# Byte offsets of TensorE's operands: activations, gate halves and split keys placed at a different offset modulo 256 in each chunk, step or pair of heads

## The chip, the cores and the metric

The kernel runs on one core of one Trainium2 chip. The metric is the device time of one execution in microseconds; the time before is the median of three runs, 678.17 us (676.92 to 685.84). The profile is one execution taken by the hardware profiler, and its span, 676.2 us, runs from the first to the last instruction.

## What is computed

Sliding-window attention with four sink keys, and behind it a two-matrix feed-forward with the gate h - tanh(h). Everything is float32.

```python
batch, n_heads, seq, head_dim = (4, 8, 768, 64)      # n_sink 4, window 128
scores = matmul(q, k.transpose(0, 1, 3, 2)) / sqrt(64)
keep = is_sink | ((rel >= 0) & (rel < window))       # rel = query position - key position
a = softmax(where(keep, scores, -1e9))
x = matmul(a, v).transpose(0, 2, 1, 3).reshape(3072, 512)
h = x @ w_in                                          # 512 x 2048
out = (h - tanh(h)) @ w_out                           # 2048 x 512
```

## The kernel before

**Tiles and stages.** The 3072 rows are cut into 12 chunks of 256 rows, and the feed-forward's 2048 columns into 8 groups of 256. A step is one chunk and one group; there are 96 steps, in an order of which chunks 0 to 2 share the first 24 (n = 0 to 23) and chunks 3 to 11 follow with eight steps each (n = 24 to 95). Attention for a chunk is done in four units, one for each pair of heads, some steps ahead of the chunk's first step.

**Split operands.** Products that have to be exact to float32 are made of single-pass products: a value is written as a high half, rounded to float32r, and a low half, the rest. A float32r product is one matmul instruction where a plain float32 product of the scores or values is two.

**The matmuls of a step.** `first_half` (mm1, L807) makes h: 24 matmuls of 128x128 stationary by 256 moving columns. Stationary is a block of w_in, from the resident tiles `w` for chunks 0 to 2, and from a ring of streamed blocks (`ring` and `spare`) for chunks 3 to 11. Moving is the chunk's activations, high half xh or low half xl, which lie in one tile `xall` (two places, by `home(cc)`) except for chunk 2, which has two tiles xh and xl of its own. `gate` (L826 to L848) takes h through tanh on ScalarE, the difference on VectorE, and writes the gate's two halves into `ghbuf` (ScalarE, L832 or L845) and `glbuf` (VectorE, L835 or L848). `second_half` multiplies them by w_out, and TensorE has the gate's halves as stationary and w_out as moving. For chunks 0 to 4 and for the last step these are 12 matmuls of 512 columns (mm2, L877). For chunks 5 to 11 they are 21 matmuls of 256 columns (mm7, L911), the seven products of a Strassen scheme on sums of the gate's and the weights' quarters.

**The attention's matmuls.** From unit 12 on, scores are two float32r passes over 260 columns (L524): moving is `ks`, the split keys of the pair, stationary is `q`. The other attention matmuls are plain float32: transposes of 128 columns (L609), and the values (L672).

**Order.** A planner (`Work`) fixes the order of all instructions of all engines from durations, due times and the resources that each piece of work names; ("gl", n % 2) is the name of a step's low half in `glbuf`. On TensorE the order is step n's L807, then step n - 1's L877 or L911, with pieces of attention between them.

**Where the operands lie.** A tile's place in SBUF, counted in bytes from its partition's start, follows from the pools. In the built program before, modulo 256: all of `w`, the Strassen weights `edge` and `w_out` blocks lie at 0, except the tile that holds w_in group 1 and later the ring, at 64 (`FAR`). `spare`, `ghbuf`, `glbuf` and `q` lie at 64. `xall` is read at 0 for chunks 3 to 11, and at 64 for chunks 0 and 1 (the `16 * (cc < 3)` in `x_high`). Chunk 2's xh is at 64 and its xl at 0. `ks` is read at 0 and 128 for the first half of a unit's queries and at 16 and 144 for the second.

```python
at = 2 * NPAIR * CH * (1 - home(cc)) + 16 * (cc < 3)
both = xall[:, at : at + 2 * NPAIR * CH].rearrange("p (k n c) -> p k n c", k=2, n=NPAIR)
```

Of the kernel before, what the change touches and what calls it, by code (L numbers as in the profile page):

```python
# [39 lines left out]
@with_exitstack  # L40
def kernel(
    ctx: ExitStack,
    tc: tile.TileContext,
    qd: bass.AP,
    kp: bass.AP,
    vp: bass.AP,
    vs: bass.AP,
    nsw: bass.AP,
    w_in: bass.AP,
    w_out: bass.AP,  # L50
    xd: bass.AP,
    out: bass.AP,
):
    nc = tc.nc

    cpool = ctx.enter_context(tc.tile_pool(name="cpool", bufs=1))
    ident = cpool.tile([P, P], F32, tag="ident", name="ident")
    nswi = cpool.tile([P, 32], I32, tag="nswi", name="nswi")[:, :4]

    pts = cpool.tile([P, NPAIR, 2, 4, P], F32, tag="pt", name="pt")  # L60
    early = []
    for m in range(2):
        first = pts[:, m].rearrange("p h a b -> p (h a b)")
        early.append((first[:, :KW], first[:, KW : KW + 2 * CH].rearrange("p (h s) -> p h s", h=2)))
    et = mybir.EngineType
    with tc.manual_schedule(engines={et.PE, et.SP, et.DVE, et.Activation, et.Pool}):

        scr = pts[:, 2, 0]
        nc.sync.dma_start(nswi, nsw.partition_broadcast(P))
        for m in range(2):  # L70
            k, q = early[m]
            nc.sync.dma_start(k, kp[0, m, :, :KW])
            _load_pair(nc, q, qd[0, 2 * m : 2 * m + 2, :, :CH], True)
            if m == 0:
                make_identity(nc, ident)
                nc.gpsimd.iota(scr[:, 0, :].bitcast(I32), pattern=[[-1, P]], base=0, channel_multiplier=1)
                nc.gpsimd.iota(scr[:, 1, :].bitcast(I32), pattern=[[1, P]], base=0, channel_multiplier=0)
        masks = _masks(nc, cpool, nswi, scr)
        _, (nlo, nhi, wlo, whi) = nc.values_load_multi_w_load_instructions(
            nsw[0:1, 0:4], skip_runtime_bounds_check_because="every value takes one of the two branches"  # L80
        )
        bad = nhi | whi | ((nlo + 3) >> 3) | ((wlo - 1) >> 7)


        WARM = 3
        with tc.tile_pool(name="warm", bufs=1, space=PSUM) as wp:
            warm = wp.tile([P, P], F32, tag="warm", name="warm")
            for _ in range(WARM):
                nc.tensor.matmul(warm, lhsT=ident, rhs=ident, start=True, stop=True)

    with tc.If(bad == 0) as cmp:
        _banded(tc, qd, kp, vp, vs, masks, w_in, w_out, ident, pts, early, out)
    with cmp.Else():
        _general(tc, qd, kp, vp, nswi, w_in, w_out, ident, xd, out)

# [8 lines left out]
        nc.sync.dma_start(q[r, h, :], src[h, r])  # L104


def _masks(nc, pool, nswi, scr):

    mask = pool.tile([P, 3, TS], F32, tag="mask", name="mask")
    above = pool.tile([P, P], F32, tag="above", name="above")
    below = pool.tile([P, P], F32, tag="below", name="below")
    after = pool.tile([P, P], F32, tag="after", name="after")
    lim = pool.tile([P, 2], F32, tag="lim", name="lim")
    diff, col, tmp = (scr[:, i, :] for i in range(3))
    nc.gpsimd.memset(mask[:, 0, :NSK], NEG)
    nc.vector.tensor_copy(diff, diff.bitcast(I32))
    nc.vector.tensor_copy(col, col.bitcast(I32))  # L120
    nc.vector.tensor_scalar(above, diff, 0.0, None, op0=ALU.is_lt)
    nc.vector.tensor_scalar(below, diff, 0.0, None, op0=ALU.is_le)
    nc.vector.tensor_scalar(after, diff, 0.0, None, op0=ALU.is_gt)
    nc.vector.scalar_tensor_tensor(diff, above, float(P), diff, op0=ALU.mult, op1=ALU.add)
    nc.vector.tensor_scalar(tmp, above, NEG, None, op0=ALU.mult)
    nc.vector.tensor_copy(lim[:, 0:1], nswi[:, 0:1])
    nc.vector.tensor_copy(lim[:, 1:2], nswi[:, 2:3])
    n_sink, window = lim[:, 0:1], lim[:, 1:2]
    nc.vector.tensor_scalar(mask[:, 2, NSK:], diff, window, NEG, op0=ALU.is_ge, op1=ALU.mult)
    nc.vector.tensor_scalar(col, col, n_sink, NEG, op0=ALU.is_ge, op1=ALU.mult)  # L130
    nc.vector.tensor_tensor(mask[:, 0, NSK:], mask[:, 2, NSK:], tmp, op=ALU.min)
    nc.vector.tensor_tensor(mask[:, 0, NSK:], mask[:, 0, NSK:], col, op=ALU.max)

    near, edge, sink = diff[:, :NSK], tmp[:, :NSK], col[:, :NSK]
    nc.vector.tensor_scalar(near, near, window, None, op0=ALU.is_lt)
    nc.vector.tensor_tensor(edge, edge, near, op=ALU.mult)
    nc.vector.tensor_tensor(mask[:, 1, :NSK], edge, sink, op=ALU.min)

    def rest():
        nc.scalar.copy(mask[:, 1, NSK:], mask[:, 2, NSK:])  # L140
        nc.scalar.copy(mask[:, 2, :NSK], sink)

    return mask, above, below, after, rest
# [86 lines left out]
        return sorted(start, key=lambda n: (start[n], n)), start  # L230


def _banded(tc, qd, kp, vp, vs, masks, w_in, w_out, ident, pts, early, out):
    nc = tc.nc
    et = mybir.EngineType
    with ExitStack() as ctx:
# [6 lines left out]
        bpool, wmpool, qpool, kpool, hpool, xpool = (  # L243
            pool(n, 1) for n in ("bpool", "wmpool", "qpool", "kpool", "hpool", "xpool")
        )
        pp, sm = pool("pp", 2), pool("sm", 4)
        xall = xpool.tile([P, 4 * NPAIR * CH + 16], F32R, tag="xall", name="xall")
        ps, ps_h = pool("ps", 1, space=PSUM), pool("ps_h", 2, space=PSUM)
        dpool = pool("dpool", 1, space=bass.MemoryType.DRAM)

        banks = {n: ps.tile([P, 512], F32, tag=n, name=n) for n in ("s0", "s1", "o0", "o1", "t", "x")}
# [4 lines left out]
        flat = wide.rearrange("p a b c -> p (a b c)")  # L256
        gbuf = gpool.tile([P, 8, P], F32, tag="gbuf", name="gbuf")
        ghbuf = gpool.tile([P, 2, 7, P], F32R, tag="ghbuf", name="ghbuf")
        glbuf = gpool.tile([P, 8, P], F32R, tag="glbuf", name="glbuf")
        wscr = dpool.tile([NG, P, 2 * WG], F32, tag="wscr", name="wscr")  # L260
        bscr = dpool.tile([NG, P, 5, DM // 2], F32, tag="bscr", name="bscr")
        kscr = dpool.tile([2, P, 2, DM // 2], F32, tag="kscr", name="kscr")
# [33 lines left out]
        def home(cc):  # L296

            return cc if cc < 3 else cc % 2

        def raw(u):  # L300
            return u < RAW
# [111 lines left out]

        sides = cpool.tile([P, 4], F32, tag="sides", name="sides")
        sidei = cpool.tile([P, 16], I32, tag="sidei", name="sidei")[:, :4]
        half, odd = sides[:, 0:2], sides[:, 2:4]
        vsink = cpool.tile([P, 2, P], F32R, tag="vsink", name="vsink")
        vraw = cpool.tile([P, P], F32, tag="vraw", name="vraw")  # L420
# [53 lines left out]
        def split(u):  # L474

            def k_high(h):
                if h == 0:
                    t = hpool.tile([P, NPAIR * CH], F32R, tag="ha", name=f"ks{u}")  # L480
                    ks[u] = t[:, : 2 * (KW + 24)].rearrange("p (h k) -> p h k", h=2)[:, :, :KW]
                r = slice(64 * h, 64 * h + 64)
                nc.scalar.copy(ks[u][r, h, :], kt[u][r, :])  # L483

            def k_low(h):
                k, t = ks[u], kt[u]
                r, o = slice(64 * h, 64 * h + 64), slice(64 * (1 - h), 64 * (1 - h) + 64)
                (nc.gpsimd if KP else nc.vector).tensor_tensor(k[o, h, :], t[r, :], k[r, h, :].bitcast(F32), op=ALU.subtract)  # L488

            def q_high():  # L490
                t = bpool.tile([P, 2, 2, CH], F32R, tag="hb", name=f"q{u}")
                qh[u], ql[u] = t[:, 0], t[:, 1]
                nc.scalar.copy(qh[u], qt[u])

            def q_low():
                (nc.gpsimd if QP else nc.vector).tensor_tensor(ql[u], qt[u], qh[u].bitcast(F32), op=ALU.subtract)  # L496

            t = due_unit(u) - 5000
            k, q = ([s] for s in slots(u))
            old = [("x", 2)] + [("xu", 2, i) for i in range(NPAIR)] if u == 3 * NPAIR else []  # L500
            work.add("ACT", 525, t, q_high, q, ["qh"] + old)
            work.add("POOL" if QP else "DVE", 1360 if QP else 705, t, q_low, q + ["qh"], ["ql"], port=True)
            for h in range(2):
                work.add("ACT", 425, t, lambda h=h: k_high(h), k, [("ks", h)] + old)
                work.add("POOL" if KP else "DVE", 1050 if KP else 590, t, lambda h=h: k_low(h), k, [("ks", h)], port=True)

        def scores(u, t):
# [21 lines left out]
            def merge():  # L529
                ps = sps[u, t]  # L530
                if t == 0:
                    if slot(u) > 1:
                        pr[u] = wide[:, slot(u) - 2]
                    else:
                        pr[u] = pp.tile([P, 4, TS], F32, tag="p", name=f"p{u}")
                    st[u] = sm.tile([P, 12], F32, tag="st", name=f"st{u}")
                for h in range(2):
                    if kind > 0:
                        nc.vector.copy_predicated(ps[h][:, TS:WIN], above.bitcast(U32), ps[h][:, :P])
# [102 lines left out]
        def attend(cc, p0, pairs):  # L642
# [35 lines left out]
            def x_high(i):  # L678
                if p0 == 0 and i == 0:
# [1 line left out]
                        xh[cc] = bpool.tile([P, NPAIR, CH], F32R, tag="hb", name=f"xh{cc}")  # L681
                        xl[cc] = hpool.tile([P, NPAIR, CH], F32R, tag="ha", name=f"xl{cc}")
                    else:
                        at = 2 * NPAIR * CH * (1 - home(cc)) + 16 * (cc < 3)
                        both = xall[:, at : at + 2 * NPAIR * CH].rearrange("p (k n c) -> p k n c", k=2, n=NPAIR)
                        xh[cc], xl[cc] = both[:, 0], both[:, 1]
                r = slice(p0 + 2 * i, p0 + 2 * i + 2)
# [126 lines left out]

        def halves(n):
            r = n % 2
            return ghbuf[:, r].rearrange("p b t -> p (b t)")[:, : 2 * CH], glbuf.rearrange("p b t -> p (b t)")[:, r * 2 * CH : (r + 1) * 2 * CH]

        def gate(n):
            g0 = gbuf.rearrange("p b t -> p (b t)")[:, : 2 * CH]  # L820
# [542 lines left out]
```

## Time and profile before

| | |
|---|---|
| time, median of 3 runs | 678.17 us (676.92 to 685.84) |
| the profiled execution: its span | 676.2 us |
[...]
| matmul records | 5099 |
| HBM traffic over the span | 225 GB/s |

The profile gives no time of its own for the profiled execution beside its span; the median of the runs is 1.97 us above it. A matmul's recorded duration is the time from its start until its last result; matmuls overlap in the pipeline, so the rate at which TensorE works is not read from the duration but from the distance between starts, and where a row merges several matmuls, from the start of the next row less the start of this one, divided by the count.

### The profile page before, as it was taken

Reading aid. Unit: us, or ns where it says so; the run is one execution under the profiler, and the core shown is the slowest. Engines: PE = TensorE matmul, PEld = TensorE weight load, DVE = VectorE, ACT = ScalarE, POOL = GpSimd, SP = SyncE. Lnnn points to the kernel's source line nnn. Section 1 sums busy time; section 2 is a strip of 40 time slices with the busy share of each in tenths; the row PEclk is TensorE's granted clock in tenths of the full one; section 3 lists DMA queues with packets and bytes.
Section 4 is the critical chain, followed back from the end, with each engine's and each line's share of the span. In section 5 each row is a group of like instructions: output and inputs, shape, how many; then the busy total and the mean of one; then the engine's idle time right before and its main releaser. Section 6 shows DMA issues by size and latency. Waiting matters only on the chain.

```text
span 676.2 us, 14570 instructions
## 1 busy us (share of the span) xinstructions
PE 655.5 (97%) x5099; PEld 603.3 (89%) x5099; DVE 531.8 (79%) x1365; ACT 412.6 (61%) x1056; POOL 204.0 (30%) x363
## 2 busy tenths in 40 slices
PE   6899999999999999999999999999999999999995
PEld 4677899998988899889999999999999999999995
DVE  6889998964898975567798898888988878855654
ACT  4986443435998876556776667567667567632331
POOL 5454000001995443344523323332223322300100
PEclk9999999999999999999999999999999999999998
DMA  5878797786998677799977767867777766657861
GB/s 177 266 262 269 266 295 263 270 287 175 191 203 274 203 217 223 227 280 266 300 217 240 224 199 207 260 196 203 227 231 216 242 199 199 198 165 207 270 198 37
DMA packets 79341, 152.96 MB, mean 226 GB/s; under 512 B 9564, under 2 KB 25564, under 8 KB 79260
## 3 DMA queue, kind: packets, MB, share of 16 engines
q1 hardware_dynamic: 65884, 121.65, 57.4%
q0 software_dynamic: 13376, 30.30, 16.4%
q8 instruction: 42, 0.69, 0.4%
q14 instruction: 39, 0.32, 0.1%
HBM read 131.47 MB, written 20.45 MB: 225 GB/s over the span
## 4 chain that ended last, share of the span: by engine, by line
PE 73%; ACT 7%; DVE 5%; DMA 5%; POOL 4%; issue 4%; POOLq 0%; SPq 0%; DVEq 0%; ACTq 0%
PE h L807 30%; PE s L911 10%; PE o L911 7%; PE o L877 6%; PE x L672 3%; PE s L877 3%; DMA w<-bscr 2%; PE t L609 2%; PE t L672 2%; PE t L877 2%; PE t L524 2%; PE x L877 2%; ACT p L575 2%; PE x L524 1%; ACT p L549 1%
## 5 line engine op out<-in xcount | busy, mean ns | idle before, releaser
L807 PE MATMUL h<-xall,ring 128*128 128x256 f32 x990 | 130.9, 279 | 0.0
L807 PEld LDWEIGHTS h<-xall,ring 128*128 128x128 f32 x990 | 121.2, 188 | 0.9 <-PE t L672 0.2
L826 ACT ACTIVATE gbuf<-h 128x512 f32<-128x512 f32 x96 | 57.1, 595 | 84.6 <-PE h L807 55.2
L356 POOL DMA_DIRECT2D qraw<-qd x36 | 29.3, 813 | 222.4 <-DVE q L496 198.0
L807 PE MATMUL h<-xall,spare 128*128 128x256 f32 x738 | 96.2, 277 | 0.0
L807 PEld LDWEIGHTS h<-xall,spare 128*128 128x128 f32 x738 | 90.0, 188 | 0.5
L549 ACT ACTIVATE p<-p,st 128x132 f32<-128x132 f32 x168 | 66.9, 400 | 26.8 <-DVE st L541 25.5
L845 ACT CAST ghbuf<-gbuf 128x896 fp32r<-128x896 f32 x55 | 51.9, 943 | 49.3 <-DVE gbuf L842 48.8
L848 DVE TENSOR_TENSOR glbuf<-gbuf,ghbuf 128x896 fp32r<-128x896 f32 x55 | 60.3, 1096 | 19.7 <-ACT ghbuf L845 16.0
L575 ACT ACTIVATE p<-p,st 128x132 f32<-128x132 f32 x168 | 54.2, 394 | 3.9 <-DVE st L570 3.5
L829 DVE TENSOR_TENSOR gbuf<-h,gbuf 128x512 f32<-128x512 f32 x55 | 37.8, 687 | 19.1 <-ACT gbuf L826 18.7
L877 PE MATMUL o<-w,ghbuf 128*128 128x512 f32 x192 | 50.8, 399 | 0.3
L629 POOL TENSOR_TENSOR pt<-pt,after 128x512 f32<-128x512 f32 x32 | 44.4, 1386 | 22.0 <-ACT pt L626 21.3
L807 PE MATMUL h<-xall,w 128*128 128x256 f32 x384 | 50.5, 282 | 0.0
L807 PEld LDWEIGHTS h<-xall,w 128*128 128x128 f32 x384 | 48.5, 188 | 1.6
L829 DVE TENSOR_TENSOR h<-h,gbuf 128x512 f32<-128x512 f32 x41 | 28.5, 694 | 19.1 <-ACT gbuf L826 19.0
L488 DVE TENSOR_TENSOR ks<-kraw,ks 64x392 fp32r<-64x392 f32 x72 | 40.4, 562 | 3.4 <-ACT ks L483 1.1
L877 PEld LDWEIGHTS o<-w,ghbuf 128*128 128x128 f32 x192 | 33.8, 188 | 6.8 <-ACT ghbuf L832 0.9
L623 DVE TENSOR_TENSOR pt<-t,below 128x512 f32<-128x512 f32 (+1 forms) x48 | 28.8, 600 | 12.6 <-PE t L609 7.4
L483 ACT CAST ks<-kraw 64x392 fp32r<-64x392 f32 x72 | 37.1, 515 | 2.2 <-DMA kraw<-kp 1.4
L911 PE MATMUL s<-edge,ghbuf 128*128 128x256 f32 x220 | 35.5, 280 | 0.1
L835 DVE TENSOR_TENSOR glbuf<-h,ghbuf 128x512 fp32r<-128x512 f32 x41 | 28.1, 685 | 9.1 <-ACT ghbuf L832 9.1
(174 smaller groups left out, 1560.8 us busy)
## 6 DMA issues: line engine op xcount, KB each, us to landing
ring<-wscr SPq DMA_DIRECT2D x165, 256.0 KB, 4.3
spare<-wscr SPq DMA_DIRECT2D x123, 256.0 KB, 4.6
qraw<-qd POOLq DMA_DIRECT2D x36, 256.0 KB, 5.0
wraw<-w_in SPq DMA_DIRECT2D x16, 512.0 KB, 6.0
wraw<-w_out SPq DMA_DIRECT2D x16, 512.0 KB, 5.7
wscr<-w SPq DMA_DIRECT2D x16, 512.0 KB, 6.0
kraw<-kp POOLq DMA_DIRECT2D x36, 196.0 KB, 4.6
v<-vp POOLq DMA_DIRECT2D x18, 256.0 KB, 3.4
```

The source lines that it names most:

```text
L483: nc.scalar.copy(ks[u][r, h, :], kt[u][r, :])
L488: (nc.gpsimd if KP else nc.vector).tensor_tensor(k[o, h, :], t[r, :], k[r, h, :].bitcast(F32), op=ALU.subtract)
L549: nc.scalar.activation(e, e, AF.Exp, bias=st[u][:, j : j + 1], scale=-1.0, accum_out=st[u][:, 4 + j : 5 + j],)
L575: nc.scalar.activation(pr[u][:, j, :], pr[u][:, j, :], AF.Copy, scale=s[:, 8 + j : 9 + j])
L629: nc.gpsimd.tensor_tensor(w[:, :, 0, :], w[:, :, 0, :], after.unsqueeze(1).to_broadcast([P, 4, P]), op=ALU.mult)
L807: nc.tensor.matmul(hps[n][:, f, :], lhsT=w, rhs=x, start=r == 0, stop=r == 11)
L826: nc.scalar.activation(g0, h(), AF.Tanh)
L829: nc.vector.tensor_tensor(g0 if strassen(n) else h(), h(), g0, op=ALU.subtract)
L845: nc.scalar.copy(ghbuf[:, n % 2], gbuf[:, 1:, :])
L848: nc.vector.tensor_tensor(glbuf[:, :7, :], gbuf[:, 1:, :], ghbuf[:, n % 2].bitcast(F32), op=ALU.subtract)
L877: nc.tensor.matmul(sums_of(n, cc, t), lhsT=a[:, f, t * P : (t + 1) * P], rhs=wt[1, g][:, (0, 1, 0)[i], f, :], start=first and not low and ...
L911: nc.tensor.matmul(acc, lhsT=a[:, b, :], rhs=factor(g, m, part % 2), start=g == 0 and part == 0 and m in (4, 1, 2, 7), stop=closes(n) and ...
```

## The change

No instruction is added, removed or moved: on every engine the same operations stand in the same order. What changes is where operands lie.

- **Activations**, `xoff(cc)`: `xall` is read, in bytes modulo 256, at 192 for chunk 0, 160 for 1, 0 for 3 (as before), 192 for 4, 16 for 5, 176 for 6, 32 for 7, 160 for 8, 48 for 9, 112 for 10 and 0 for 11 (as before). Chunk 2 is not in `xall`. The stationary blocks that go with them stay at 64, or 0 and 64 for chunks 0 and 1.
- **The gate's halves** of the 512-column steps, `shift(n)`: `ghbuf` and `glbuf` are used 0, 32, 64, 96 or 128 bytes further on, by n modulo 5. The moving weights stay at 0. The Strassen steps keep 64 and 0.
- **Split keys**: `ks` of unit u begins 32 * (u % 8) bytes further on, and the second head of the pair lies a multiple of 256 bytes behind the first, so that TensorE reads them at 32 * (u % 8) and 16 more.
- To make room, `lim`, `sides`, `sidei` and one of the four `st` buffers move into the unused columns of the tile of `nswi`, the other `st` share one tile, and `glbuf` moves to another pool and grows by 128 bytes.

```diff
-        xall = xpool.tile([P, 4 * NPAIR * CH + 16], F32R, tag="xall", name="xall")
+        SHIFT, XOFF = 32, 48
+        xall = xpool.tile([P, 4 * NPAIR * CH + XOFF], F32R, tag="xall", name="xall")
...
+        stats = sm.tile([P, 3, 12], F32, tag="st", name="st")
+        glflat = cpool.tile([P, SHIFT + 8 * P], F32R, tag="glbuf", name="glbuf")
+        glbuf = glflat[:, : 8 * P].rearrange("p (b t) -> p b t", b=8)
...
+        def xoff(cc):
+            return (48, 40, 0, 0, 48, 4, 44, 8, 40, 12, 28, 0)[cc]
+
+        def shift(n):
+            return (0, 8, 16, 24, 32)[n % 5]
...
-                    ks[u] = t[:, : 2 * (KW + 24)].rearrange("p (h k) -> p h k", h=2)[:, :, :KW]
+                    o = 8 * (u % 8)
+                    ks[u] = t[:, o : o + 896].rearrange("p (h k) -> p h k", h=2)[:, :, :KW]
...
-                    st[u] = sm.tile([P, 12], F32, tag="st", name=f"st{u}")
+                    st[u] = stats[:, u % 4] if u % 4 < 3 else small[:, 20:32].bitcast(F32)
...
-                        at = 2 * NPAIR * CH * (1 - home(cc)) + 16 * (cc < 3)
+                        at = 2 * NPAIR * CH * (1 - home(cc)) + xoff(cc)
...
             r = n % 2
-            return ghbuf[:, r].rearrange("p b t -> p (b t)")[:, : 2 * CH], glbuf.rearrange("p b t -> p (b t)")[:, r * 2 * CH : (r + 1) * 2 * CH]
+            a, b = shift(n), shift(n) + r * 2 * CH
+            return ghbuf[:, r].rearrange("p b t -> p (b t)")[:, a : a + 2 * CH], glflat[:, b : b + 2 * CH]
```

One thing follows from the last hunk. The low halves of two steps in a row lay side by side in `glbuf`; with shifts that differ they overlap by up to 32 columns, so the write of one can have to wait until TensorE has read the other. The order of VectorE's low halves (L835 before, L847 now) from step 4 on, first in the kernel before:

```order
244 L835 TENSOR_TENSOR glbuf<-h_1050,ghbuf 128x512 [waits Activation_49]
...
247 L835 TENSOR_TENSOR glbuf<-h_1101,ghbuf 128x512 [waits Activation_49]
...
253 L835 TENSOR_TENSOR glbuf<-h_1157,ghbuf 128x512 [waits Activation_49]
```

and in the changed one, at the same places:

```order
244 L847 TENSOR_TENSOR glbuf<-h_1036,ghbuf 128x512 [waits Activation_49]
...
247 L847 TENSOR_TENSOR glbuf<-h_1087,ghbuf 128x512 [waits PE_49,Activation_49]
...
253 L847 TENSOR_TENSOR glbuf<-h_1143,ghbuf 128x512 [waits PE_49,Activation_49]
```

Nothing moved; 15 of the 41 low halves of this form have a wait for TensorE (PE) more.

## Rows read from the trace of the kernel before

**Rows 1.** The page: span, and busy time of TensorE and VectorE
```profile
span 676.2 us, 14570 instructions
...
PE 655.5 (97%) x5099; PEld 603.3 (89%) x5099; DVE 531.8 (79%) x1365; ACT 412.6 (61%) x1056; POOL 204.0 (30%) x363
```

**Rows 2.** The page: the chain that ended last, by engine and by line
```profile
PE 73%; ACT 7%; DVE 5%; DMA 5%; POOL 4%; issue 4%; POOLq 0%; SPq 0%; DVEq 0%; ACTq 0%
PE h L807 30%; PE s L911 10%; PE o L911 7%; PE o L877 6%; PE x L672 3%; PE s L877 3%; DMA w<-bscr 2%; PE t L609 2%; PE t L672 2%; PE t L877 2%; PE t L524 2%; PE x L877 2%; ACT p L575 2%; PE x L524 1%; ACT p L549 1%
```

**Rows 3.** Waits of TensorE, longest first: total us, times, longest
```profile
PE s L517 <- DMA qk<-qd: 3.3, 2, 1.7
PE warm L89 <- POOL pt L103: 3.2, 1, 3.2
```

**Rows 4.** Line 807: duration ns min/median/max, first and last start us
```profile
L807 PE MATMUL h<-xall,ring x990: 276/276/388, 205.0 to 663.5; 128*128 128x256 f32 x198
...
L807 PE MATMUL h<-xall,spare x738: 276/276/374, 209.1 to 662.8; 128*128 128x256 f32 x185
...
L807 PE MATMUL h<-xall,w x384: 276/279/472, 42.6 to 192.7; 128*128 128x256 f32 x192
```

**Rows 5.** The chain in order of time: start us, us, what
```profile
98.88 2.86 PE h L807 x24
...
104.53 2.83 PE h L807 x24
...
159.06 2.80 PE s L877 x12
...
364.32 3.40 PE h L807 x30
```

**Rows 6.** Timeline of TensorE, 595 to 600 us: start us, us, instructions
```profile
594.98 1.52 PE L807 MATMUL h<-xall,ring 128*128 128x256 f32 x12
596.34 0.84 PE L807 MATMUL h<-xall,spare 128*128 128x256 f32 x6
597.02 0.62 PE L911 MATMUL s<-edge,ghbuf 128*128 128x256 f32 x4
...
599.40 0.84 PE L807 MATMUL h<-xall,spare 128*128 128x256 f32 x6
```

**Rows 7.** Timeline of TensorE, 489 to 496 us
```profile
489.71 3.09 PE L807 MATMUL h<-xall,ring 128*128 128x256 f32 x24
492.64 0.40 PE L524 MATMUL t<-ks,q 128*128 128x260 f32 x2
...
493.12 0.63 PE L911 MATMUL s<-edge,ghbuf 128*128 128x256 f32 x4
493.59 0.39 PE L911 MATMUL o<-edge,ghbuf 128*128 128x256 f32 x2
493.81 0.62 PE L911 MATMUL s<-w,ghbuf 128*128 128x256 f32 x4
...
494.72 0.40 PE L524 MATMUL t<-ks,q 128*128 128x260 f32 x2
...
495.21 0.41 PE L911 MATMUL s<-edge,glbuf 128*128 128x256 f32 x2
```

**Rows 8.** Timeline of TensorE, 143 to 147 us, steps of 512 columns
```profile
143.37 0.63 PE L877 MATMUL x<-w,glbuf 128*128 128x512 f32 x2
143.84 2.03 PE L877 MATMUL s<-w,ghbuf 128*128 128x512 f32 x8
145.70 0.63 PE L877 MATMUL s<-w,glbuf 128*128 128x512 f32 x2
```

**Rows 9.** Timeline of VectorE, the same stretch
```profile
143.66 0.68 DVE L835 TENSOR_TENSOR glbuf<-h,ghbuf 128x512 fp32r<-128x512 f32 x1
144.27 1.21 DVE L735 TENSOR_TENSOR w<-pt,w 128x1024 fp32r<-128x1024 f32 x1
```

More of the change, by code (lines that the diff above doesn't have):

```diff
@@ L57 @@
     ident = cpool.tile([P, P], F32, tag="ident", name="ident")
-    nswi = cpool.tile([P, 32], I32, tag="nswi", name="nswi")[:, :4]
+    small = cpool.tile([P, 32], I32, tag="nswi", name="nswi")
+    nswi = small[:, :4]
     pts = cpool.tile([P, NPAIR, 2, 4, P], F32, tag="pt", name="pt")
@@ L77 @@
                 nc.gpsimd.iota(scr[:, 1, :].bitcast(I32), pattern=[[1, P]], base=0, channel_multiplier=0)
-        masks = _masks(nc, cpool, nswi, scr)
+        masks = _masks(nc, cpool, small, scr)
         _, (nlo, nhi, wlo, whi) = nc.values_load_multi_w_load_instructions(
@@ L91 @@
     with tc.If(bad == 0) as cmp:
-        _banded(tc, qd, kp, vp, vs, masks, w_in, w_out, ident, pts, early, out)
+        _banded(tc, qd, kp, vp, vs, small, masks, w_in, w_out, ident, pts, early, out)
     with cmp.Else():
@@ L104, in _load_pair, with _masks @@
         nc.sync.dma_start(q[r, h, :], src[h, r])
-def _masks(nc, pool, nswi, scr):
+def _masks(nc, pool, small, scr):
     mask = pool.tile([P, 3, TS], F32, tag="mask", name="mask")
@@ L115, in _masks @@
     after = pool.tile([P, P], F32, tag="after", name="after")
-    lim = pool.tile([P, 2], F32, tag="lim", name="lim")
+    nswi, lim = small[:, :4], small[:, 4:6].bitcast(F32)
     diff, col, tmp = (scr[:, i, :] for i in range(3))
@@ L230, in order, with _banded @@
         return sorted(start, key=lambda n: (start[n], n)), start
-def _banded(tc, qd, kp, vp, vs, masks, w_in, w_out, ident, pts, early, out):
+def _banded(tc, qd, kp, vp, vs, small, masks, w_in, w_out, ident, pts, early, out):
     nc = tc.nc
@@ L245, in _banded @@
         )
-        pp, sm = pool("pp", 2), pool("sm", 4)
-        xall = xpool.tile([P, 4 * NPAIR * CH + 16], F32R, tag="xall", name="xall")
+        pp, sm = pool("pp", 2), pool("sm", 1)
+        SHIFT, XOFF = 32, 48
+        xall = xpool.tile([P, 4 * NPAIR * CH + XOFF], F32R, tag="xall", name="xall")
         ps, ps_h = pool("ps", 1, space=PSUM), pool("ps_h", 2, space=PSUM)
+        stats = sm.tile([P, 3, 12], F32, tag="st", name="st")
+        glflat = cpool.tile([P, SHIFT + 8 * P], F32R, tag="glbuf", name="glbuf")
+        glbuf = glflat[:, : 8 * P].rearrange("p (b t) -> p b t", b=8)
         dpool = pool("dpool", 1, space=bass.MemoryType.DRAM)
@@ L258, in _banded @@
         ghbuf = gpool.tile([P, 2, 7, P], F32R, tag="ghbuf", name="ghbuf")
-        glbuf = gpool.tile([P, 8, P], F32R, tag="glbuf", name="glbuf")
         wscr = dpool.tile([NG, P, 2 * WG], F32, tag="wscr", name="wscr")
@@ L412, in _banded @@
             qt[u], kt[u] = q, k
-        sides = cpool.tile([P, 4], F32, tag="sides", name="sides")
-        sidei = cpool.tile([P, 16], I32, tag="sidei", name="sidei")[:, :4]
+        sides = small[:, 8:12].bitcast(F32)
+        sidei = small[:, 16:20]
         half, odd = sides[:, 0:2], sides[:, 2:4]
```

## The prediction, made before the changed kernel ran

> **What bounds the kernel now.** I read the page's busy times first: TensorE is busy 655.5 of 676.2 us [rows 1], so little of its time is idle. Then the chain that ended last: 73% of it is TensorE, and 30% of the span is line 807 alone [rows 2]. Then TensorE's waits: the two longest totals are 3.3 and 3.2 us [rows 3]. So for most of the span the kernel lasts as long as TensorE takes to work off its queue, and a change of the time per matmul passes into the end nearly one to one. VectorE, busy 531.8 us [rows 1], is next.
>
> Since no instruction moves, the question is whether the time per matmul depends on where its operands lie. Durations give the first sign: line 807 shows 276 ns at least everywhere, and 276 is also the median on `ring` and `spare`, but on `w` the median is 279 [rows 4]. The distances between starts say more. With moving data at 0 and stationary at 64 (modulo 256), 30 matmuls in a row take 3.40 us, 113.3 ns each [rows 5]; so do the 18 from 594.98 to 597.02 (2.04 us) and the 21 of line 911 behind them, up to 599.40 (2.38 us) [rows 6]. With moving at 64 and stationary at 0, the 24 at 104.53 take 2.83 us, 117.9 ns; with both halves at different places (chunk 2: 64 and 0, against 0), the 24 at 98.88 take 2.86 us, 119.2 ns [rows 5]. [...]
>
> The good level isn't held by the placing alone. At 489.71, behind the attention's value products, 24 matmuls at the good offsets take 2.93 us, 122.1 ns; behind four of line 524, the next four of line 911 take 0.47 us, 117.5 ns, and the two after them 0.22 us, 110 ns by the row's two decimals [rows 7]. So TensorE has to fall into the good level after a disturbance, mostly within a handful of matmuls, sometimes only after a whole step. I read this as a lock between the two operands' reads that exists at 0 against 64, and that no row here shows at another placing.
>
> **The change, part by part.**
>
> *Activations, chunks 4 to 10*: 7 chunks x 8 steps x 24 = 1344 matmuls of line 807 leave the good placing. Upper bound from rows of matmuls with the operands elsewhere: 122.5 ns, the four of line 524 from 494.72 to 495.21 with moving at 16 and 144 [rows 7] (their 260 columns make them 1.6% longer by themselves, 120.6 ns for 256). Nearer is the range 117.9 to 119.2 ns of line 807 itself [rows 5]. Lower bound: the best that any row shows, 113.3. I take 118, near the row of the same form: 118 - 113.3 = 4.7 ns more for those that are at the good level now. That is not all of them; the median of 276 ns in rows 4 says over half, rows 6 and 7 show steps of either kind, and I estimate 0.8. So 1344 x 0.8 x 4.7 ns = 5.1 us. Bounds: from 1344 x 0.2 x -4.7 = -1.3 us (every one comes to the good level) to 1344 x (120.6 - 113.3) x 0.9 = +8.8 us, and with a price that no row shows, more (a rival below).
>
> *Line 911* keeps its own offsets, but now each of its groups follows matmuls that are out of step. Rows 7 show the price of falling in again, 4 x (117.5 - 113.3) = 17 ns; over the 48 steps of chunks 5 to 10 that is 0.8 us. Bounds 0 and, if the lock is not found in 21 matmuls, 48 x 21 x 4.5 ns = 4.5 us.
>
> *Chunks 0 and 1*: 384 matmuls go from 64 to 192 and 160. Chunk 0 then has the same distance between its operands as the good placing (192 - 0, as 0 - 64), so it could gain 192 x 4.6 ns = 0.9 us; chunk 1 I leave as it is. Since each step there is broken by matmuls of 512 columns, I take -0.2, with bounds of -1.8 (both chunks gain) and +0.9 us.
>
> *Gate halves, 480 matmuls of 512 columns less those at shift 0*: now 232.5 ns (eight in 1.86 us) [rows 8] to 233.3 ns (twelve in 2.80) [rows 5]. Twice the two levels of 256 columns is 226.7 and 236; present matmuls are already between them, so I take 0, with bounds of 384 x -6 = -2.3 us and 384 x +3 = +1.2 us.
>
> *Split keys, 288 matmuls of 260 columns*: 120.0 ns now at 0 and 128 (0.48 us for four) and 122.5 at 16 and 144 [rows 7]. The new offsets are half of either kind; 0, with bounds of -1.4 us (to 113.3 x 260/256 = 115.1) and +0.7.
>
> *The added waits*: 15 low halves on VectorE wait for a read by TensorE. At step 15 the low half starts at 143.66 [rows 9]; the two 512-column matmuls that read the old values start at 143.37 and end 0.63 us later, 144.00 [rows 8]: a delay of 0.34 us, behind which line 735 (1.21 us) [rows 9] queues. The reader of the new values starts at 145.70 [rows 8], 1.36 us after the low half's end at 144.34. So TensorE is still served in time, and I take 0. Were that cover gone, 15 x 0.34 = 5.1 us.
>
> *Small tiles* hold the same instructions without further waits: 0.
>
> Sum: 5.1 + 0.8 - 0.2 = +5.7 us on a span of 676.2, so 681.9. The runs' median stands 678.17 - 676.2 = 2.0 us above the profiled span, which gives 683.9; I say 683.5, since a little will go into TensorE's few waits.
>
> [...] The two levels in rows 5 and 6 do not agree with a rate that depends on columns alone.
>
> **The rivals.**
>
> [...] The two levels would be owed to the sequence of the work: chunks 0 to 2 are broken by matmuls of 512 columns, chunks 4 to 11 are not. For it: steps at 0 against 64 also run slowly after a disturbance [rows 7]. Against it: 24 in a row at 104.53 never come to 113 [rows 5], where four were enough in rows 7. Then line 807 stays and the time is 678.2, between 677 and 680.
>
> [...]
>
> *Faster.* The lock exists at several of the new distances, and chunks 0, 1 and the 512-column steps find it too: -1.3 - 1.8 - 2.3 - 1.4 = -6.8 us, so 671.4. Against it: the good level seems a floor, 276 ns being the minimum on all tiles in rows 4, so 2% (13.6 us) is out of reach unless a better level exists.
>
> *The waits cost.* If VectorE's delays reach TensorE, 5.1 us on top of the forecast, 689.
>
> **How the numbers follow.** The forecast (offsets cost some 4 to 6 ns on line 807) has 0.57, no effect 0.22, faster 0.08, waits that cost 0.04, slower by over 2% 0.09. The forecast's own range is 680.5 to 688. For 8 in 10 I go down to 676, which takes in most of the case without effect, and up to 692. A measurement here tells a change of 2% from none; so faster 0.01, same 0.90, slower 0.09.
>
> **What would show it.** In the changed profile: line 807 on `ring` and `spare` with a median of 280 or more in place of 276, steps of chunks 4 to 10 at 2.83 us or more for 24, and chunks 3 and 11, whose offsets stay, still at 2.72 us; line 911 with its first four matmuls of a group slow; line 847 with short waits for TensorE, and TensorE with none for `glbuf`. I am wrong if chunks 4 to 10 still run at 113.3 ns, if some of these chunks go below it, or if TensorE's waits grow.

## The result, and the profile after

| | before | after |
|---|---|---|
| median | 678.59 us (20 runs, 676.33 to 685.84) | 683.35 us (20 runs, 681.38 to 684.44) |
| ratio, 95% interval | | 1.0056 [1.0041, 1.0072] |
| profiled execution: its time, its span | -, 676.2 us | 682.59 us, 680.8 us |
| TensorE in it, mean granted clock, as a share of full speed | 0.997 | 0.999 |

The changed kernel is slower by 0.56%, 4.8 us by the medians. The forecast was 683.5 us. The page, with the chain that ended last, against [rows 1, 2]:

```profile
span 680.8 us, 14583 instructions
...
PE 661.3 (97%) x5099; PEld 610.5 (90%) x5099; DVE 531.8 (78%) x1365; ACT 412.8 (61%) x1056; POOL 203.8 (30%) x363
...
PE 82%; ACT 4%; DVE 4%; POOL 3%; DMA 3%; issue 2%; SPq 0%; POOLq 0%; DVEq 0%; ACTq 0%
PE h L818 35%; PE s L923 11%; PE o L923 8%; PE o L889 8%; PE x L683 3%; PE s L889 3%; PE t L620 2%; PE t L683 2%; PE t L535 2%; PE t L889 2%; PE x L535 2%; PE x L889 2%; PE s L535 1%; DMA v<-vp 1%; DMA kraw<-kp 1%
```

VectorE and ScalarE are as busy as before; TensorE has 5.8 us more, with the same 5099 instructions, and its share of the chain grew from 73% to 82%. The 13 instructions that the page has more are semaphore waits of VectorE. Line 807 is line 818 now (911 is 923, 877 is 889, 524 is 535, 609 is 620). Its durations, with columns as in [rows 4]:

```profile
L818 PE MATMUL h<-xall,ring x990: 274/281/386, 204.0 to 668.1; 128*128 128x256 f32 x198
...
L818 PE MATMUL h<-xall,spare x738: 274/281/369, 208.2 to 667.4; 128*128 128x256 f32 x185
...
L818 PE MATMUL h<-xall,w x384: 274/281/472, 41.7 to 191.9; 128*128 128x256 f32 x192
```

The median on `ring` and `spare` went from 276 to 281 ns. The rate is read from distances between starts, in TensorE's timeline, as in [rows 6 to 8]:

```profile
142.36 0.62 PE L889 MATMUL x<-w,glbuf 128*128 128x512 f32 x2
142.82 2.03 PE L889 MATMUL s<-w,ghbuf 128*128 128x512 f32 x8
144.69 0.63 PE L889 MATMUL s<-w,glbuf 128*128 128x512 f32 x2
...
392.74 0.87 PE L818 MATMUL h<-xall,ring 128*128 128x256 f32 x6
393.45 2.23 PE L818 MATMUL h<-xall,spare 128*128 128x256 f32 x18
395.54 0.62 PE L923 MATMUL s<-edge,ghbuf 128*128 128x256 f32 x3
...
607.38 1.58 PE L818 MATMUL h<-xall,ring 128*128 128x256 f32 x12
608.80 1.58 PE L818 MATMUL h<-xall,spare 128*128 128x256 f32 x12
610.23 0.64 PE L923 MATMUL s<-edge,ghbuf 128*128 128x256 f32 x4
...
660.09 2.99 PE L818 MATMUL h<-xall,ring 128*128 128x256 f32 x24
662.91 0.63 PE L923 MATMUL s<-edge,ghbuf 128*128 128x256 f32 x4
```

A step of chunk 10 (activations at 112) takes 2.85 us from 607.38 to 610.23, 118.8 ns a matmul, where a matmul of chunk 10 took 113.3 in [rows 6]. A step of chunk 6 (at 176) begins slowly, 6 in 0.71 us, and goes on with 18 in 2.09, 116.1 ns each. Chunk 11, whose offset did not change, takes 2.82 us for 24 at 660.09, 117.5 ns; that was not expected. The eight 512-column matmuls at 142.82, which keep their place (shift 0), take 1.87 us, where eight took 1.86 in [rows 8].

How the loss is spread is seen when each matmul's start is taken from the start of the next one and the differences are summed by line; the sums cover the time from the first matmul to the last. Second column: another profile of the kernel before.

```
us               before   before, again   after
L807/818         272.52      273.49      277.81
L911/923         134.86      135.59      136.28
L877/889         116.55      116.57      116.22
L524/535          38.33       39.19       38.15
L609/620          22.61       22.80       20.97
others            81.52       82.15       81.54
sum              666.39      669.79      670.97
```

The two profiles of the same kernel differ by 3.4 us, spread over all rows but line 877; the medians are the better measure of the whole. Line 807's increase is larger than the difference between the two profiles.

And by chunk: the mean distance to the next start on line 807/818, over distances under 135 ns (longer ones hold a wait or other work; 184 to 191 of 192 remain in each chunk).

```
chunk                       0      1      2      3      4      5      6      7      8      9     10     11
before: offset             64     64   64, 0     0      0      0      0      0      0      0      0      0
before: ns              117.9  117.8  118.9  114.5  114.6  114.4  114.2  113.9  114.8  114.3  113.7  113.4
after: offset             192    160   64, 0     0    192     16    176     32    160     48    112      0
after: ns               116.2  118.5  118.6  116.1  118.6  118.9  116.8  118.3  119.4  117.5  118.3  116.1
```

Chunks 4 to 10 rise from a mean of 114.3 to 118.2 ns. In what follows, "the good distance" is the one between moving data at 0 and stationary data at 64, 192 modulo 256, and "the good level" is 113.3 ns.

### The profile page after: what moved, and what is told of

The parts are those of the page before. It is cut to its first block, busy times and chain, and to the rows that moved or that the text cites. A ratio compares the mean times of both kernels' runs of the same rounds, so it can differ in the third digit from the quotient of the medians.

```text
span 680.8 us, 14583 instructions
## 1 busy us (share of the span) xinstructions
PE 661.3 (97%) x5099; PEld 610.5 (90%) x5099; DVE 531.8 (78%) x1365; ACT 412.8 (61%) x1056; POOL 203.8 (30%) x363
## 4 chain that ended last, share of the span: by engine, by line
PE 82%; ACT 4%; DVE 4%; POOL 3%; DMA 3%; issue 2%; SPq 0%; POOLq 0%; DVEq 0%; ACTq 0%
PE h L818 35%; PE s L923 11%; PE o L923 8%; PE o L889 8%; PE x L683 3%; PE s L889 3%; PE t L620 2%; PE t L683 2%; PE t L535 2%; PE t L889 2%; PE x L535 2%; PE x L889 2%; PE s L535 1%; DMA v<-vp 1%; DMA kraw<-kp 1%
## 5 line engine op out<-in xcount | busy, mean ns | idle before, releaser
L818 PE MATMUL h<-xall,ring 128*128 128x256 f32 x990 | 134.3, 282 | 0.1
L818 PEld LDWEIGHTS h<-xall,ring 128*128 128x128 f32 x990 | 123.9, 188 | 1.0 <-issue 0.3
L818 PE MATMUL h<-xall,spare 128*128 128x256 f32 x738 | 98.9, 281 | 0.0
L818 PEld LDWEIGHTS h<-xall,spare 128*128 128x128 f32 x738 | 92.2, 188 | 0.5
L560 ACT ACTIVATE p<-p,st 128x132 f32<-128x132 f32 x132 | 52.6, 401 | 21.3 <-DVE st L552 20.3
L586 ACT ACTIVATE p<-p,st 128x132 f32<-128x132 f32 x132 | 42.6, 394 | 2.9 <-DVE st L581 2.5
L847 DVE TENSOR_TENSOR glbuf<-h,ghbuf 128x512 fp32r<-128x512 f32 x41 | 28.1, 686 | 10.0 <-ACT ghbuf L844 7.7
```

The source lines that it names most:

```text
L560: nc.scalar.activation(e, e, AF.Exp, bias=st[u][:, j : j + 1], scale=-1.0, accum_out=st[u][:, 4 + j : 5 + j],)
L586: nc.scalar.activation(pr[u][:, j, :], pr[u][:, j, :], AF.Copy, scale=s[:, 8 + j : 9 + j])
L818: nc.tensor.matmul(hps[n][:, f, :], lhsT=w, rhs=x, start=r == 0, stop=r == 11)
```

## The experiments

Two theories to begin with. A: the distance between the two operands' places, modulo 256 bytes, sets the time of a matmul, and line 807 carries nearly the whole loss. B: it does not; the loss is in the halves' and keys' offsets, in the added waits, or in the moving operand's own place. All experiments but one repeated profile are edits of the changed kernel, so its small tiles stay where they are; "old" halves and keys are these two lines:

```diff
-            return (0, 8, 16, 24, 32)[n % 5]
+            return 0
...
-                    o = 8 * (u % 8)
-                    ks[u] = t[:, o : o + 896].rearrange("p (h k) -> p h k", h=2)[:, :, :KW]
+                    o = 0
+                    ks[u] = t[:, o : o + 2 * (KW + 24)].rearrange("p (h k) -> p h k", h=2)[:, :, :KW]
```

**Activations alone, and everything but the activations.** The first has old halves and keys. The second is the changed kernel with

```diff
-            return (48, 40, 0, 0, 48, 4, 44, 8, 40, 12, 28, 0)[cc]
+            return 16 * (cc < 3)
```

> The changed kernel with the gate's halves and the split keys back at their old offsets; the activations stay at the new ones. Theory (line 807's price per matmul in chunks 0 to 10 is the whole loss, and what it disturbs): 682 to 684 us, ratio to before 1.005 to 1.008, chunks 4 to 10 at 117 to 119.5 ns a matmul, as in the changed kernel. Rival (the added waits of VectorE or the halves' offsets carry a good part of it): under 681 us. Chunk 3, which keeps its offsets, tells who spoiled it in the changed kernel: back at 114.5 ns if the halves or keys did, 116 if not.

> The complement: activations at their old offsets, halves and keys at the new ones, with the added waits. Theory: 678 to 680 us, ratio 0.999 to 1.002; chunks 4 to 11 near 114 ns. Rival (halves, keys or waits cost): over 681 us.

Measured: activations alone 1.0039 [1.0023, 1.0055] (683.73 us beside 680.61), the rest alone 0.9980 [0.9963, 0.9997] (679.79 beside 680.61). The loss is the activations'; halves, keys and the added waits cost nothing, and if anything that kernel is 0.2% faster. The ratio of the first lies below the range expected, its time within it: the kernel before took 680.61 us in this series and 678.59 beside the changed kernel. The two parts' ratios do not make up the whole's 1.0056 either, so some 2 us between series of runs have to be allowed for. With activations alone, chunks 4 to 10 show 118.6, 119.1, 116.9, 118.2, 119.4, 117.5 and 118.4 ns, each within 0.3 ns of the changed kernel. One stretch in chunk 5 of that profile is not in its mean: TensorE stood for 1.95 us until VectorE was done (line 552), and then its granted clock was 0.50 of full speed from 342.8 to 346.2 us, with over 200 ns from one matmul of line 818 to the next. Chunk 3 came back to 114.8 ns, against 115.8 with the new halves and keys; both are near enough to the 114.5 and 115.1 of two profiles of the kernel before that I conclude nothing from it.

The added waits are there. VectorE's waits in the profile of the changed kernel:

```profile
DVE glbuf L847 <- PE o L889: 1.0, 1, 1.0
...
DVE glbuf L847 <- PE s L889: 0.8, 1, 0.8
...
DVE glbuf L847 <- PE x L889: 0.3, 1, 0.3
```

Three of them lasted, 2.1 us together. The third is the one the prediction worked out, at step 15; VectorE's timeline there:

```profile
141.55 1.22 DVE L746 TENSOR_TENSOR w<-pt,w 128x1024 fp32r<-128x1024 f32 x1
143.09 0.69 DVE L847 TENSOR_TENSOR glbuf<-h,ghbuf 128x512 fp32r<-128x512 f32 x1 [0.32 <-PE x L889]
143.70 1.22 DVE L746 TENSOR_TENSOR w<-pt,w 128x1024 fp32r<-128x1024 f32 x1
```

0.32 us, where 0.34 was forecast, and its reader on TensorE starts at 144.69, 0.91 us after its end. TensorE's own waits for the low halves, in the kernel before and in the changed one:

```profile
PE t L877 <- DVE glbuf L835: 0.8, 1, 0.8
...
PE t L889 <- DVE glbuf L847: 0.7, 1, 0.7
```

**Everything 64 bytes up.** Old halves, keys and activations, and a pad ahead of all tiles, so that the places of the feed-forward's operands move and their distances stay. `xall` gives up 128 bytes that it does not need here, so the tiles `p` and `st` move 64 bytes down instead.

```diff
+    cpool.tile([P, 16], F32, tag="pad", name="pad")
     ident = cpool.tile([P, P], F32, tag="ident", name="ident")
...
-        SHIFT, XOFF = 32, 48
+        SHIFT, XOFF = 32, 16
```

> All offsets as before, but a pad of 64 bytes at the start of SBUF moves every tile 64 bytes up: moving data at 64 and stationary at 128 for lines 807, 877 and 911, all distances unchanged. Theory A (the distance of the two operands decides): 677 to 680 us, the level of 113.3 ns in chunks 3 to 11 as before. Theory B (the moving operand has to begin at a multiple of 256): lines 807 and 911 at 117 to 119 ns throughout, 3400 matmuls by 3 to 4 ns more, 688 to 692 us.

Measured: 0.9995 [0.9973, 1.0016]. Chunks 3 to 11 run at 113.5 to 114.9 ns. Line 807 (here 819) shows the old medians with moving data at 64 and stationary at 128:

```profile
L819 PE MATMUL h<-xall,ring x990: 276/276/388, 204.4 to 665.5; 128*128 128x256 f32 x198
L819 PE MATMUL h<-xall,spare x738: 276/276/374, 208.5 to 664.8; 128*128 128x256 f32 x185
```

So the distance decides, not where the moving operand begins. Theory B is out.

**One chunk alone.** Old halves and keys, and chunk 10 at 112 as the only new offset:

```diff
-            return (48, 40, 0, 0, 48, 4, 44, 8, 40, 12, 28, 0)[cc]
+            return 28 if cc == 10 else 16 * (cc < 3)
```

> All offsets as before, except that chunk 10's activations are at 112. In the changed kernel chunk 11 is slower than before though its own offsets are the same. Theory (the good level is a state that lasts from one matmul to the next and has to be found again once it is lost): chunk 10 at 118 ns a matmul and chunk 11, behind it, at about 116 with whole steps at 117.7, all other chunks as before. Rival (something else in the changed kernel slows chunk 11, such as where small tiles lie): chunk 11 stays at 113.3 ns.

Measured: chunk 10 at 118.4, chunk 11 at 116.7 ns, as my theory had it. But it does not hold: with activations alone, chunk 10 has the same 112 and chunk 11 runs at 113.3; and with everything but the activations, chunk 10 has the good distance and chunk 11 runs at 116.7. What chunk 10 does is not what slows chunk 11.

**The same kernels once more.** So I profiled two kernels a second time, the one before, and the one with chunks 0 and 1 at 192 (below).

> The kernel before, unchanged, for a second profile. In its first profile chunk 11 ran at the good level throughout, 113.35 ns a matmul; in three of the experiments the same offsets gave 116.1 to 117.8 there. Theory (the good distance has two levels, and which one an execution falls into behind the last attention work is chance): chunk 11 can be at either, 113.3 or 116 to 118 ns, and chunks 4 to 9 differ from the first profile by some tenths. Rival (the program's layout decides): chunk 11 again at 113.3 to 113.4 and the other chunks within 0.1 ns of their first means.

> The kernel with chunks 0 and 1 at 192, unchanged, for a second profile; in its first, chunks 10 and 11 ran at 116.7 and 117.8 ns. Theory (chance of the execution): another mix, chunk 11 at 113.3 or between. Rival (the layout decides): chunk 11 at 117.8 again. Chunks 0 and 1, with the good distance, at 115.8 to 116.0 again in either case.

Measured, chunks 10 and 11 of the kernel before: 113.7 and 113.4 ns in the first profile, 116.7 and 115.0 in the second. Of the other kernel: 116.7 and 117.8, then 113.5 and 116.1. The second profile of the kernel before, in a step of chunk 10:

```profile
606.89 1.58 PE L807 MATMUL h<-xall,ring 128*128 128x256 f32 x12
608.31 1.58 PE L807 MATMUL h<-xall,spare 128*128 128x256 f32 x12
609.72 0.63 PE L911 MATMUL s<-edge,ghbuf 128*128 128x256 f32 x4
```

24 matmuls in 2.83 us, 117.9 ns, with the program, offset and chunk of [rows 6], where it was 113.3. At the good distance TensorE has two levels, 113.3 and 117.8 ns, and which of them it runs at is not the same in two profiles of one program. For the kernel with chunks 0 and 1 at 192 the two profiles come from two chips, so a difference between chips is not ruled out; but both levels stand within one execution too. In chunk 11 of the changed kernel, which keeps the good distance, three steps run at the good level and the other five at the slow one:

```profile
633.47 2.20 PE L818 MATMUL h<-xall,ring 128*128 128x256 f32 x18
635.51 0.84 PE L818 MATMUL h<-xall,spare 128*128 128x256 f32 x6
636.19 0.62 PE L923 MATMUL s<-edge,ghbuf 128*128 128x256 f32 x4
...
649.49 0.87 PE L818 MATMUL h<-xall,spare 128*128 128x256 f32 x6
650.19 2.28 PE L818 MATMUL h<-xall,ring 128*128 128x256 f32 x18
652.31 0.63 PE L923 MATMUL s<-edge,ghbuf 128*128 128x256 f32 x4
```

24 matmuls take 2.72 us, then 2.82. The clock is not what differs: in the window view of the same profile TensorE's granted clock, behind the busy time and the count, is 1.00 in both stretches.

```profile
628.00:641.00 13.00, 13.00 (x116) 1.00 0.77 225
642.00:668.00 26.00, 26.00 (x223) 1.00 0.57 188
```

The level changes there across a break: one distance of 409 ns, at 641.23 us. In the second profile of the kernel before it changes the other way, from the slow level to the good one, across a distance of 164 ns at 641.52. Other changes come without such a break, so what brings the stream from one level to the other is not settled. The sums by line above show what it may be worth: 1.0 us on line 807 and 0.7 us on line 911 between two profiles of one program.

**The new offsets dealt out anew, and other distances.** Old halves and keys, and

```diff
-            return (48, 40, 0, 0, 48, 4, 44, 8, 40, 12, 28, 0)[cc]
+            return (48, 40, 0, 0, 28, 12, 48, 4, 44, 8, 40, 0)[cc]
```

or `(48, 48, 0, 0, 36, 16, 32, 20, 24, 24, 28, 0)`.

> The seven new offsets of chunks 4 to 10 dealt out anew: 112, 48, 192, 16, 176, 32 and 160 for chunks 4 to 10; halves and keys at their old offsets. Theory (the distance sets the mean time of a matmul of line 807): the means go with the offset, within 0.6 ns of what the changed kernel showed: 112 at 118.3, 48 at 117.5, 192 at 118.6, 16 at 118.9, 176 at 116.8, 32 at 118.3, 160 at 119.4 ns, over starts less than 135 ns apart. Rival (the chunk's place in the sequence sets it): the means stay with the chunks, chunk 6 at 116.8 and chunk 8 at 119.4.

> Distances not tried yet: activations of chunks 4 to 10 at 144, 64, 128, 80, 96, 96 and 112, stationary at 64, so 80, 0, 64, 16, 32, 32 and 48 bytes apart. Theory: each distance but 192 and, in part, 112 lies at 117 to 119.5 ns; the two chunks at 32 agree within 0.6 ns; a distance of 64 is at 117.7 as chunks 0 and 1 were before. Rival (another distance holds the good level too, or a better one): a chunk at 113.3 ns or less. Chunks 0 and 1 both at 192 against 0: 116 ns each.

Measured, first: 112 at 118.3, 48 at 117.5, 192 at 118.8, 16 at 118.9, 176 at 117.1, 32 at 118.1, 160 at 119.5 ns. Each mean goes with its offset to within 0.4 ns, whatever chunk it is in. Second: the two chunks at a distance of 32 agree (116.9 and 117.0), and none comes to 113.3; distance 64 is at 117.9 as expected. Together, the mean time of a matmul of line 807 in chunks 3 to 11 by the distance from stationary to moving, modulo 256 bytes:

```
distance      0     16     32     48     64     80     96    112    128    192    208    224    240
ns        119.3  117.2  116.9  118.3  117.9  118.7  119.4  116.8  118.6  113.3  118.9  118.2  117.5
up to                                             119.7  117.1  118.8  117.8  119.1
```

Distances 144, 160 and 176 were not tried in chunks 3 to 11. 192 is the best, and the only one whose mean varies by more than half a nanosecond between chunks and runs. At 112, 40 to 47% of a chunk's matmuls are at 113 or 114 ns, at no other new distance more than 24%. That 256 bytes is the period was taken for granted and not tested by itself.

**The good distance for chunks 0 and 1.** Old halves and keys, and

```diff
-            return (48, 40, 0, 0, 48, 4, 44, 8, 40, 12, 28, 0)[cc]
+            return 48 if cc < 2 else 0
```

> All offsets as before, but chunks 0 and 1 at 192 in place of 64, which against stationary data at 0 is the good distance. Theory: both at 116 ns in place of 117.9, 2 x 192 x 1.9 ns = 0.7 us, ratio to before 0.999, hardly clear of noise. Rival (the gain is taken by waits of the weights' preparation in the first 200 us): no change.

Measured: both chunks at 115.8 and 116.0 ns in place of 117.9 and 117.8, in both profiles, as expected; the time 1.0006 [0.9982, 1.0029]. One of the eight groups of either chunk stands at 128 there, since its stationary block lies at 64, and chunk 0 of the changed kernel, whose other groups are at 192 too, shows the two levels again: 113.5 ns in the mean of the step at 155.05 us, 117.9 in that at 189.21. 0.7 us is too little to be told from no change here, and in the first profile the slow level of chunks 10 and 11 cost more than that. This is the version that the distances point to; it beats the changed kernel and is not measurably better than the one before.

**The dearest offset everywhere.** Old halves and keys, and chunks 3 to 11 all at 160:

```diff
-            return (48, 40, 0, 0, 48, 4, 44, 8, 40, 12, 28, 0)[cc]
+            return 40 if cc > 2 else 16 * (cc < 3)
```

> The dearest offset, 160 against 64, for all of chunks 3 to 11, and nothing else. Theory (TensorE's time per matmul passes into the end one to one): 1728 matmuls of line 807 from about 114.3 to 119.4 ns are 8.8 us, with 0.8 to 1.5 us for line 911, so 9.6 to 10.3 us on top of before, a ratio of 1.013 to 1.016. Rival (other engines set the pace of some steps, so part of it is hidden): under 6 us, a ratio under 1.009.

Measured: 1.0087 [1.0058, 1.0116], 3.9 to 7.9 us; its middle, 5.9 us, is the rival's figure, not mine. All nine chunks run at 119.4 to 119.7 ns; a step of chunk 10:

```profile
608.65 1.59 PE L818 MATMUL h<-xall,ring 128*128 128x256 f32 x12
610.08 1.60 PE L818 MATMUL h<-xall,spare 128*128 128x256 f32 x12
611.52 0.64 PE L923 MATMUL s<-edge,ghbuf 128*128 128x256 f32 x4
```

2.87 us for 24. By the means, chunks 3 to 11 pay 1728 x (119.5 - 114.2) = 9.2 us against the first profile of the kernel before, and 8.2 against the second (114.7); the time shows less, so it seems that part of the loss does not reach the end. Where it goes is not shown. By line, against the first profile: line 807 takes 280.40 us, +7.9; line 911 135.38, +0.5; line 524 37.49, -0.8; line 609 20.43, -2.2. It looks as if 3.0 us came back on two attention lines, whose matmuls stand in front of work of other engines. But in the six profiles in which chunks 3 to 11 all stand at the good distance, line 609 takes anything from 20.40 to 22.80 us and line 524 from 37.99 to 39.19, so these two differences cannot be put down to the offset. My expectation took the passage as one to one; that is where it erred.

## Why the prediction was right, and where it was not

**The bound** was read rightly: line 807 takes 5.3 us more against the first profile of the kernel before and 4.3 against the second, the median of the runs rose by 4.8, and no other engine became busier. The share of the chain says little about it: 82% here, but anything from 70 to 80% in the six profiles at the good distance.

**Activations, chunks 4 to 10**, forecast +5.1 us at 118 ns for 0.8 of 1344 matmuls. The mean after is 118.2 ns, and the sums of these seven chunks are 161.3 us against 156.6, +4.7. Every chunk went up, and no offset was free. The price of 118 ns and the share of 0.8 were both near what was measured: 118 - 0.8 x 4.7 = 114.2 ns, where the mean before is 114.3. The rival that owes the two levels to the sequence of the work, with 678.2 us, is shown wrong by the experiments with activations alone (1.0039) and everything else alone (0.9980), and by the permuted offsets, whose means go with the offset to within 0.4 ns.

**Line 911**, forecast +0.8, is +1.4 us against the first profile and +0.7 against the second. It cannot be told from what differs between executions.

**Chunks 0 and 1**, forecast -0.2: -0.1. Chunk 0 gained 1.7 ns a matmul at the good distance, chunk 1 lost 0.7 at another.

**Gate halves and keys**, forecast 0: -0.3 and -0.2 us. The halves' distance matters too, and not in the order of the table above. Twelve 512-column matmuls of one step, at distance 192 before and at 64 (shift 4) in the changed kernel:

```profile
84.63 2.03 PE L877 MATMUL s<-w,ghbuf 128*128 128x512 f32 x8
86.50 1.09 PE L877 MATMUL s<-w,glbuf 128*128 128x512 f32 x4
87.43 0.28 PE L807 MATMUL h<-xh,w 128*128 128x256 f32 x1
...
83.71 2.00 PE L889 MATMUL s<-w,ghbuf 128*128 128x512 f32 x8
85.55 1.08 PE L889 MATMUL s<-w,glbuf 128*128 128x512 f32 x4
86.46 0.28 PE L818 MATMUL h<-xh,w 128*128 128x256 f32 x1
```

They take 2.80 us before and 2.75 after. Over distances under 245 ns, the matmuls that went to 64 have a mean of 230.5 ns, and 229.8 in the kernel with everything but the activations, where the same ones took 233.2 before; at 96, 128, 160 and 192 the means are 232.2 to 234.0 in both kernels. 95 matmuls by some 3 ns are the 0.3 us of line 877, too little to be told in the time.

**The waits**, forecast 0: 2.1 us on VectorE, and TensorE's wait for line 847 is 0.7 us, where it was 0.8 for line 835. TensorE was still served in time, as worked out.

**Chunks 3 and 11** were to stay at 2.72 us for 24. That failed: 2.82 us in five of the eight steps of chunk 11, 116.1 ns in the mean of either, 0.7 us together. The step that was wrong is the sentence that at the good offsets TensorE falls in again mostly within a handful of matmuls. Two profiles of one program show that it may run at the slow level for whole steps: 24 matmuls at 117.9 ns each in the second, where the first had 113.3. Such a step stood already in [rows 7]: of the 2.93 us from 489.71, the first matmul's distance is 225 ns, and the other 23 take 117.6 ns each at the good offsets.

**Line 609** took 1.6 us less, which I had not put into the sum. That is within the 20.40 to 22.80 us that this line takes at the good distance, so it need not come from the change.

**Luck.** The forecast of 683.5 us is met to 0.2 us. The main term was right in its cause, the relative place of the operands, and in its size; whether a lock is behind it was not shown. That the total came so near is in part luck, since +0.7 us of chunks 3 and 11 were not in the sum and the medians of one program differ by some 2 us between series.

**Slower by over 2%**, which had 0.09, did not come: the dearest distance anywhere, over all nine chunks, costs 0.9%. No chunk's mean on line 807 came to the 120.6 ns that the upper bound was worked out with; the highest is 119.7 ns.

**Rival, faster**: one chunk, 6, reached stretches at 113 ns at a new distance, the rest none, and no chunk's mean went below 113.3. Single durations of 274 ns appear now on `xall`. 276 was not the floor that I took it for even before: [rows 4] leave out chunk 2, whose row shows 274 at a mean distance of 118.9 ns, so the least duration is no sign of the rate.

```profile
L807 PE MATMUL h<-xh,w x128: 274/279/388, 63.7 to 148.9; 128*128 128x256 f32 x128
```

## What to carry to other kernels

Where TensorE works without a break, look at the distance between starts of equal matmuls in several stages of the profile: if it has more than one level, see how the two operands lie relative to each other, not where each begins (both moved by 64 bytes, chunks 3 to 11 stayed at 113.5 to 114.9 ns here). Measure for each size of matmul: the distance that was best for 256 columns, 192 bytes with 113.3 ns, was not for 512, where 64 gave 230 ns and 192 gave 232 to 234. A placing found good for one pair of buffers has to be kept for every buffer that is rotated into its place; different offsets per chunk cost 4 ns in 114 on each matmul here. When two profiles of one program already differ by a microsecond or two on a line, compare levels in the same stage, take the whole from medians, and put a line's difference down to a change only when it is larger than that line's spread over profiles of unchanged stages.

## What the runs showed of the hardware

Single-pass float32r matmuls of 256 columns behind one another start 113.3 ns apart at best, and 116.8 to 119.7 ns apart in the mean at the twelve other distances between stationary and moving data that were tried. At the best distance, 192 bytes, one and the same program runs whole steps at 113.3 ns in one profile and at 117.9 in another, and the changed kernel runs steps of one chunk at 113.3 and at 117.8 ns, both at a granted clock of 1.00. Moving all the feed-forward's tiles by 64 bytes leaves the means at 113.5 to 114.9 ns. Matmuls of 512 columns take 230 ns at distance 64 and 232 to 234 at 96 to 192. Why the distance matters was not shown, nor what brings the stream from one level to the other.
